# Half of the last group's first layer, and a quarter of group 7's, by seven products of halves

## The chip, the core and the metric

The kernel runs on one core of a Trainium2 chip. Time is device microseconds of one execution; the profile is of one execution, taken by the hardware profiler. PE is TensorE (PEld are its weight loads), DVE is VectorE, ACT is ScalarE, POOL is GpSimd, SP is SyncE, which here issues DMAs.

## What is computed

Attention with a relative bias over 8 batches of 8 heads, 576 positions of 64 elements, and after it a feed-forward layer with a squared ReLU over the 4608 resulting rows of 512 elements:

```python
scores = scale * np.matmul(q, k.transpose(0, 1, 3, 2)) + bias
attn = softmax(scores)
x = np.matmul(attn, v)          # 8 x 8 x 576 x 64, then rows of 512: 4608 x 512
h = np.maximum(x @ w_in, 0.0)   # w_in 512 x 2048
out = h * h @ w_out             # w_out 2048 x 512
```

Inputs and output are float32. On the chip the matmuls take float16 and add up in float32.

## The kernel before

**An order by a planner.** The kernel doesn't emit its instructions as it goes. It first adds operations to a plan (`P.add`), each with an assumed cost per engine, what it depends on, the buffers that it takes from small rings (`Ring`, `Buf`) and a due time. Then the plan is scheduled once as a list, and the instructions are emitted in that order. The assumed costs and due times (`due`) thus decide the order on each engine's queue, but not the time on the chip: there each engine takes its queue from the front and waits on semaphores.

**Attention.** A pair is two heads of one batch (`pair(p)`, 32 of them). Its scores go to the two double banks `st` of PSUM (ring `r_set`, lines 702, 726, 751), ScalarE takes the exponential into one of three `pt` buffers (ring `r_pt`, line 713), VectorE multiplies by the bias' exponentials (line 794), and TensorE multiplies by v into the single bank `pv` (ring `r_pv`, lines 830 and 837). VectorE normalises into `x` (lines 854 and 859), and from batch 2 on SP turns x with a DMA into `xt`, where the 512 elements lie on partitions in four chunks (line 875). Each pair does so in two parts, of three and of two tiles of positions.

**The feed-forward layer.** It works on nine groups of 512 rows (`layers(g)`, g from 0 to 8). Group 7 needs the first part of batch 7's four pairs, group 8 needs all, so both come after the last scores.
- Layer 1 has 16 blocks, one for every 128 hidden columns (`f1`, line 1102): four matmuls, one per chunk of the 512 elements, each with 512 moving columns (the rows of x), into one of three banks `f` (ring `r_g`). ScalarE takes the ReLU of a block into one of four `rt` buffers (line 1123), VectorE squares it into `g` (line 1133), of which there are two, taken in turn by the groups.
- Layer 2 (`second(g)`, line 1017) already computes a product of two matrices split in halves each way by seven products instead of eight (Winograd's form of Strassen's scheme). VectorE makes the sums of g (line 972); a product is 2 x 8 matmuls with 256 moving columns; the results are gathered by VectorE in four float32 buffers `y` (line 1045, or a ScalarE copy, line 1051) and written out by SP (line 1073).
- `layers(g)` puts layer 1 of group g between the products of layer 2 of group g - 1: block i of layer 1 is due at `due + i * 2000`, a step of layer 2 1000 later (and another 7000 later in group 8).

**Buffers with a second use.** `fs`, two float32 buffers, take v in float32 for later batches; `stg`, the staging buffers of q and k, take the loaded pairs. All of that is done when group 7 begins.

Of the kernel before, what the change touches and what calls it, by code (L numbers as in the profile page):

```python
# [11 lines left out]
FP16 = mybir.dt.float16  # L12
EXPF = mybir.ActivationFunctionType.Exp
RELUF = mybir.ActivationFunctionType.Relu
COPYF = mybir.ActivationFunctionType.Copy
MULT = mybir.AluOpType.mult

# [8 lines left out]
GT = 512  # L26
# [13 lines left out]
SIX = 2  # L40
V_EARLY, V_HW = 18900.0, 2
LATE2 = 7000
T_POOL, T_DUE = 0, 0
ORDER = "k0 i0 q1 q0 v i1 o0 k1 i2 o1 o2 i3 o3"
HALF = GT // 2
# [135 lines left out]
def mm(n):  # L181
    return n / 2.4 + 2.5
# [6 lines left out]
def dve(n, rate=1.0, fix=160.0):  # L189
    return fix + n / (0.96 * rate)  # L190
# [3 lines left out]
def kernel(  # L194
# [13 lines left out]
    def io(ins):  # L208
        tc.keep_in_program_order(ins)
        return ins  # L210
# [399 lines left out]

    xt_ready, x_last = {}, {}
    x_bufs = {}

    def copy_to(engs_n, out_f, in_f, deps, bufs, due, fp16=True, dve_only=False):

# [13 lines left out]
    def pair(p):  # L629
# [63 lines left out]
        def run(jts):  # L693
            sets = [Buf(r_set) for _ in jts]

            def score():
                kt, qt = kts[qb.slot], qts[qb.slot]
                for jt, st in zip(jts, sets):
                    for e in range(2):
                        rw = ds(64 * e, 64)  # L700
                        io(
                            nc.tensor.matmul(  # L702
                                sets_ps[st.slot][:, e, :], kt[rw, ts(jt, 128)], qt[rw, 0:512],
                                start=True, stop=True,
                            )
                        )

            o = P.add({"PE": len(jts) * mm(512) + 10}, score, evac, sets + [qb, pb], T, after, "r")
            for jt, st in zip(jts, sets):

                def ex(jt=jt, st=st):
                    io(
                        nc.scalar.activation(  # L713
                            out=p5(pts[pb.slot])[:, jt, :, 0:512], in_=sets_ps[st.slot], func=EXPF, scale=SCALE
                        )
                    )

                exps[jt] = P.add({"ACT": act(1024)}, ex, [o], [st, pb], T)
# [214 lines left out]
    def sums_of_weights():  # L933
# [21 lines left out]
            done.append(o)  # L955
        return done

    def sums_of_activations(g):

        gb = g_bufs[g]  # L960
        sb_ = s_bufs[g] = {i: Buf(r_s[i]) for i in (1, 2, 4)}
        for c0 in (0, 4):
            o = None
            for to, uses in ((1, [1]), (2, [1, 2]), (4, [2, 4]), (3, [])):

                def add(to=to, c0=c0):
                    a11, a12, a21, a22 = (fourth(gb, eo, t, c0, 4) for t in range(2) for eo in range(2))
                    s = {i: ss[i][:, c0 : c0 + 4] for i in (1, 2, 4)}
                    out_, a, b_ = {
                        1: (s[1], a21, a22), 2: (s[2], a11, s[1]), 4: (s[4], a12, s[2]), 3: (a21, a21, a11)  # L970
                    }[to]
                    io(nc.vector.tensor_tensor(out=out_, in0=a, in1=b_, op=mybir.AluOpType.subtract))  # L972

                o = P.add(
                    {"DVE": dve(1024, 2.0)}, add, squares[g][2 * c0 : 2 * c0 + 8] + [o],
                    [gb] + [sb_[i] for i in uses], G0 + GP * g - 5e4,
                )
                s_done.setdefault((g, to), []).append(o)

    def second(g):  # L980
# [25 lines left out]
        for i in (int(x) for x in (P_LAST if g == NG - 1 else P_ORDER).split()):  # L1006
            bk, left, right, ns = prod[i]
            own = bk == "e" and g == NG - 1
            home = pv_ps if own else g_ps
            apart = bk == "d" and g == NG - 1  # L1010
            for s_ in range(2):
                bf = bank[f"d{s_}" if bk == "d" else bk]

                def mul(i=i, s_=s_, bf=bf, left=left, right=right, apart=apart, own=own, home=home):
                    for c in range(8):
                        io(
                            nc.tensor.matmul(  # L1017
                                home[bf.slot][:, ts(s_, HALF)], left(c, s_), right(c),
                                start=(c == 0 and (s_ == 0 or apart) and (own or i not in before)), stop=(c == 7),
                                skip_group_check=True,  # L1020
                            )
                        )

                def atom(d, i=i, s_=s_, bf=bf, ns=ns, mul=mul, own=own):
                    deps = d + [x for n in ns for x in s_done[g, n]] + squares[g]
                    deps += read_of[before[i]] if i in before and not own else []
                    deps += l_wout if i in (1, 2) else t_done
                    return P.add(
                        {"PE": 8 * mm(HALF)}, mul, deps, [bf, gb] + [sb_[n] for n in ns if n != 3], 1e6, 0.0, "f",
                    )  # L1030

                atoms.append(atom)
                if s_ == 0 and not apart:
                    continue

                def fin(o, i=i, bf=bf, s0=s_ if apart else 0, n=1 if apart else 2, own=own, home=home):
                    to, plus, where = reads[i]
                    plus = "u" if own else plus
                    cs = ds(s0 * HALF, n * HALF)

                    def ev():
                        dst, ps = ys[y[to].slot][:, cs], home[bf.slot][:, cs]
                        if plus is not None:
                            io(
                                nc.vector.scalar_tensor_tensor(  # L1045
                                    out=dst, in0=ps, scalar=OSC, in1=ys[y[plus].slot][:, cs], op0=MULT,
                                    op1=mybir.AluOpType.add,
                                )
                            )
                        elif e.eng == "ACT":  # L1050
                            io(nc.scalar.activation(out=dst, in_=ps, func=COPYF, scale=OSC))  # L1051
                        else:
                            io(nc.vector.tensor_scalar_mul(out=dst, in0=ps, scalar1=OSC))

                    deps = [o]
                    if plus == "u":
                        deps += read_of[1 if i in (2, 6) else 6]
                    if i == 6 and g == NG - 1:
                        deps += read_of[2]
                    if plus == "v":  # L1060
                        deps += read_of[5]
                    if i == 4:
                        deps += read_of[3] + read_of[5]
                    bufs = [bf, y[to]] + ([y[plus]] if plus not in (None, to) else [])
                    engs = {"DVE": dve(n * HALF)} if plus is not None else {"DVE": dve(n * HALF), "ACT": act(n * HALF)}
                    e = P.add(engs, ev, deps, bufs, 0.0)
                    read_of.setdefault(i, []).append(e)
                    if where is not None:
                        t, h = where
                        P.add(  # L1070
                            {"SP": 640.0},
                            lambda: io(
                                nc.sync.dma_start(
                                    out=rows_[t][:, s0 : s0 + n, ts(h, HALF)],
                                    in_=ys[y[to].slot][:, cs].rearrange("p (s d) -> p s d", s=n),
                                )
                            ),
                            [e], [y[to]], 0.0,
                        )

                atoms.append(fin)
        return atoms

    def layers(g):

        due = G0 + GP * g
# [2 lines left out]
        if g < NG:  # L1089
            g_bufs[g] = Buf(r_gb)  # L1090
            gb1 = g_bufs[g]
            squares[g] = []
            for nt in range(16):
                bank = Buf(r_g)

                def f1(nt=nt, bank=bank):
# [10 lines left out]
                            )  # L1107

                atoms1.append((nt, f1, bank))
        i2 = 0  # L1110
        last = None
        for i in range(16):
            if i < len(atoms1):
                nt, f1, bank = atoms1[i]
                o = P.add(
                    {"PE": 4 * mm(512)}, f1, xt_ready[g] + [l_win[nt // 4]], [bank, gb1], due + i * 2000, 0.0, "f"
                )
                f1_last[g] = o
                rb = Buf(r_rt)
# [1 line left out]
                def relu(o, bank=bank, rb=rb):  # L1121
# [4 lines left out]

                engs = {"ACT": act(512), "DVE": dve(512)} if g < RELU_DVE else {"ACT": act(512)}
                r = one_of(engs, relu, [o], [bank, rb], 0.0)
                squares[g].append(
                    P.add(  # L1130
                        {"DVE": dve(512, 2.0)},
                        lambda rb=rb, nt=nt, gb1=gb1: io(
# [64 lines left out]
```

## Time and profile before

| | us |
|---|---|
| median of four runs | 373.31 |
| the four runs | 372.51 to 373.9 |
| the profiled execution | 373.9 |
| its span | 372.1 |

The span is what the profiler records between first and last instruction; the rest of an execution's time lies around it. Busy time by stretch, in us:

| stretch | PE | weight loads | VectorE | ScalarE | GpSimd |
|---|---|---|---|---|---|
| 0 to 80 | 67.8 | 42.8 | 63.9 | 66.6 | 57.3 |
| 80 to 160 | 78.6 | 53.2 | 56.6 | 56.7 | 48.7 |
| 160 to 240 | 80.0 | 56.6 | 58.2 | 60.8 | 51.3 |
| 240 to 316 | 76.0 | 54.3 | 54.6 | 52.7 | 26.8 |
| 316 to 372.1 | 53.0 | 35.4 | 31.1 | 20.9 | 0 |

The last row is the part in which only layer 1 of groups 7 and 8 and layer 2 of groups 7 and 8 are left. Its three us without TensorE are the last reads, the last write and the program's end. The granted clock is full but for the last two us, where TensorE has nothing to do.

A row of groups reads: line, engine, operation, output<-input with shapes, count | busy us, mean ns of one | idle time of the engine before it, and what ended most of that. A matmul's mean there is from its start to its modelled end, and they overlap; what one costs in a row of them is the distance of their starts.

### The profile page before, as it was taken

What the parts mean: (1) busy time and instruction counts of PE and PEld (TensorE: products, weight loads), DVE (VectorE), ACT (ScalarE), POOL (GpSimd) and SP (SyncE); (2) the same over time, 40 slices, a digit from 0 to 9 for tenths busy, and PEclk for the clock granted to TensorE, in tenths of its full rate; (3) what the DMA queues carried; (4) which work ended last, traced back from release to release, by engine and by line L of the source; (5) the groups of instructions that cost most, each with busy time, mean ns of one, the idle gap of its engine ahead of it and who ended that gap; (6) DMA issues with size and microseconds to landing.
All of it is one profiled execution on the core that took longest, in us unless ns stands there. A gap on an engine that the chain in (4) does not pass through costs nothing.

```text
span 372.1 us, 9910 instructions
## 1 busy us (share of the span) xinstructions
PE 355.4 (96%) x3930; PEld 242.4 (65%) x3930; DVE 264.3 (71%) x594; ACT 257.6 (69%) x367; POOL 184.0 (49%) x343
## 2 busy tenths in 40 slices
PE   3978999899998999999999999999999999999996
PEld 2656455556686557877785468745876688546785
DVE  3897789867775588658965687669765885483673
ACT  4998989688574887689766887688659870574220
POOL 8898359294655676656846557667623000000000
PEclk9999999999999999999999999999999999999999
DMA  9999999595999999999999899999975112200022
GB/s 171 151 126 161 200 179 94 94 115 100 175 128 124 149 158 114 131 154 163 121 128 155 108 161 122 149 167 138 121 114 130 47 43 50 85 2 28 30 84 86
DMA packets 162292, 44.25 MB, mean 119 GB/s; under 512 B 145734, under 2 KB 162246, under 8 KB 162246
## 3 DMA queue, kind: packets, MB, share of 16 engines
q0 software_dynamic: 74208, 14.53, 51.7%
q1 hardware_dynamic: 87696, 28.80, 40.5%
q8 instruction: 31, 0.51, 0.6%
q10 hardware_dynamic: 342, 0.30, 0.3%
q14 instruction: 15, 0.12, 0.1%
HBM read 36.88 MB, written 9.44 MB: 124 GB/s over the span
## 4 chain that ended last, share of the span: by engine, by line
PE 87%; DVE 7%; DMA 3%; ACT 2%; issue 1%; ACTq 0%; DVEq 0%
PE f L1102 34%; PE f L1017 28%; PE pv L837 9%; PE st L702 8%; PE pv L830 3%; PE st L751 2%; DVE pt L794 2%; DMA xt<-x 2%; PE st L726 1%; DVE x L859 1%; DMA g<-in_q_dram 1%; PE f L657 1%; ACT pm L761 1%; DVE s L972 1%; PE f L359 1%
## 5 line engine op out<-in xcount | busy, mean ns | idle before, releaser
L713 ACT ACTIVATE pt<-st 128x1024 f16<-128x1024 f32 x128 | 127.4, 1023 | 30.8 <-PE st L702 30.7
L1102 PE MATMUL f<-xt,w_in_sb 128*128 128x512 f16 (+4 forms) x704 | 138.7, 341 | 1.4 <-DMA xt<-x 1.2
L1123 ACT ACTIVATE rt<-f 128x512 f16<-128x512 f32 x144 | 85.2, 601 | 50.5 <-PE f L1102 45.4
L1102 PEld LDWEIGHTS <-w_in_sb 128*128 128x128 f16 x704 | 62.6, 98 | 57.3 <-issue 12.7
L1133 DVE TENSOR_TENSOR g<-rt 128x512 f16<-128x512 f16 x144 | 63.5, 446 | 37.7 <-ACT rt L1123 36.9
L794 DVE TENSOR_TENSOR pt<-pt,tb_sb 128x1536 f16<-128x1536 f16 (+2 forms) x96 | 59.7, 631 | 14.9 <-ACT pt L713 14.1
L1017 PEld LDWEIGHTS <-g 128*128 128x128 f16 x576 | 54.5, 98 | 14.5 <-issue 4.7
L276 POOL DMA_DIRECT2D qs<-in_q_dram x79 | 55.4, 715 | 5.0 <-DMA w_out_sb<-in_moe_w_out_dram 2.6
L276 POOL DMA_DIRECT2D ks<-in_k_dram x79 | 55.4, 704 | 1.5 <-issue 1.3
L837 PE MATMUL pv<-va,pt 128*128 128x65 f16 x1280 | 54.7, 193 | 0.0
L837 PEld LDWEIGHTS <-pt 128*128 128x128 f16 x1280 | 50.2, 97 | 3.2 <-issue 1.3
L1017 PEld LDWEIGHTS <-s 128*128 128x128 f16 x432 | 41.2, 98 | 11.1 <-issue 4.0
L1045 DVE SCALAR_TENSOR_TENSOR y<-f,y 128x512 f32<-128x512 f32 (+1 forms) x47 | 31.4, 667 | 23.4 <-PE f L1017 23.0
L702 PE MATMUL st<-qt,kt 64*128 64x512 f16 x256 | 40.7, 389 | 0.9 <-ACT pt L736 0.4
L684 POOL COPY qz<-kt 64x64 f16<-64x64 f16 x58 | 17.2, 297 | 44.6 <-DMA kt<-ks 36.1
L684 POOL COPY qz<-qt 64x64 f16<-64x64 f16 x61 | 19.6, 322 | 37.0 <-DMA qt<-qs 25.9
L830 PE MATMUL pv<-vm,pm 128*128 128x130 f16 x160 | 35.3, 221 | 1.1 <-DVE x L859 1.0
L1017 PE MATMUL f<-wt,g 128*128 128x256 f16 x288 | 36.2, 273 | 0.0
L1017 PE MATMUL f<-w_out_sb,s 128*128 128x256 f16 x288 | 36.1, 273 | 0.0
L1017 PE MATMUL f<-w_out_sb,g 128*128 128x256 f16 x272 | 34.5, 273 | 0.7 <-ACT y L1051 0.7
L859 DVE TENSOR_TENSOR x<-pv,r 128x384 f16<-128x384 f32 x64 | 31.4, 491 | 2.0
L972 DVE TENSOR_TENSOR s<-g,s 128x1024 f16<-128x1024 f16 x36 | 25.6, 712 | 0.4
(66 smaller groups left out, 283.9 us busy)
## 6 DMA issues: line engine op xcount, KB each, us to landing
out_dram<-y SPq DMA_DIRECT2D x34, 256.0 KB, 2.3
f<-in_v_dram SPq DMA_DIRECT2D x24, 256.0 KB, 4.2
qs<-in_q_dram POOLq DMA_DIRECT2D x48, 64.0 KB, 4.3
ks<-in_k_dram POOLq DMA_DIRECT2D x48, 64.0 KB, 3.5
w_in_sb<-in_moe_w_in_dram POOLq DMA_DIRECT2D x4, 512.0 KB, 7.9
w_out_sb<-in_moe_w_out_dram POOLq DMA_DIRECT2D x4, 512.0 KB, 11.6
qs<-in_q_dram POOLq DMA_DIRECT2D x7, 144.0 KB, 4.7
ks<-in_k_dram POOLq DMA_DIRECT2D x7, 144.0 KB, 6.2
```

The source lines that it names most:

```text
L276: lambda: io(eng.dma_start(out=out_(), in_=in_())),
L684: io(eng.tensor_copy(out=dst[qb.slot][rw, rw], in_=src[qb.slot][rw, 512:576]))
L702: nc.tensor.matmul(sets_ps[st.slot][:, e, :], kt[rw, ts(jt, 128)], qt[rw, 0:512], start=True, stop=True,)
L713: nc.scalar.activation(out=p5(pts[pb.slot])[:, jt, :, 0:512], in_=sets_ps[st.slot], func=EXPF, scale=SCALE)
L794: io(nc.vector.tensor_tensor(out=a, in0=a, in1=t, op=MULT))
L830: nc.tensor.matmul(ps[:, i, :, :], pm[:, c : c + 128], vm[:, hp, :, 0:65], start=True, stop=False)
L837: nc.tensor.matmul(ps[:, i, e, :], pt[:, (2 * jt + e) * S + c : (2 * jt + e) * S + c + 128], va[:, jt, 2 * hp + e, 0:65], start=False, sto ...
L859: nc.vector.tensor_tensor(out=xs[xb.slot][:, qt0 : qt0 + nq, :].rearrange("p t (e d) -> p t e d", e=2), in0=ps[:, :, :, 0:64], in1=rs[rb.s ...
L1017: nc.tensor.matmul(home[bf.slot][:, ts(s_, HALF)], left(c, s_), right(c), start=(c == 0 and (s_ == 0 or apart) and (own or i not in before ...
L1102: nc.tensor.matmul(g_ps[bank.slot][:, a:z], w_in_sb[:, kk, ts(nt, 128)], xt_sb[:, kk, c : c + z - a], start=(kk == 0), stop=(kk == 3),)
L1123: io(nc.scalar.activation(out=rts[rb.slot], in_=g_ps[bank.slot], func=RELUF))
L1133: nc.vector.tensor_tensor(out=gs[gb1.slot][:, nt, :], in0=rts[rb.slot], in1=rts[rb.slot], op=MULT)
```

## The change

The 2048 hidden columns are taken as two halves of 1024, and each half as four pieces of 256. A unit u is piece u of both halves, for one group: the four blocks 2u, 2u + 1, 8 + 2u and 9 + 2u. Group 7 computes one unit by seven products, group 8 two; the other blocks (12 and 8) stay as they were.

In a unit the 512 elements are split in halves (k), the 512 rows in halves (j), and the columns by half of the hidden layer (i). VectorE makes four sums of the group's x (`t`, once for a group, into the staging buffers of q and k) and four sums of w_in (`s_`, once for each u, into a `pt` buffer that the plan takes after the last scores). A product is four matmuls with 256 moving columns. The seven go to four banks: 1 and then 2 on top of it into one of the double banks `st`, 6 into an `f` bank, 5 and then 3 on top of it into `pv`, 7 and then 4 into the other `st`. Before a product is added to a bank, the value that the bank holds is read (ScalarE copies 1; VectorE reads 6, 5, 7, 3 and 4 and adds a float32 buffer, an `fs` or a `y`, to each). Four of the reads give quarters of the unit: 2 (read with the ReLU by ScalarE) and 7, 3 and 4 (written by VectorE to `rt`, where ScalarE takes the ReLU in place). The square of a quarter is made by VectorE or ScalarE, as the plan chooses.

`squares[g]` becomes a list for each block, so that the sums for layer 2 wait for their own blocks. Remaining blocks d of a group with units are due at `place(d)`.

```diff
+UNITS = {7: 1, 8: 2}
+AT = (0, 0.5, 2, 2.5, 4, 5.5, 7)
...
+    def made(g, a, z):
+        return [x for nt in range(a, z) for x in squares[g][nt]]
...
-                    {"DVE": dve(1024, 2.0)}, add, squares[g][2 * c0 : 2 * c0 + 8] + [o],
+                    {"DVE": dve(1024, 2.0)}, add, made(g, 2 * c0, 2 * c0 + 8) + [o],
...
+    def sum_of_w(i, u):
+        return pts[late["room"].slot][:, ts(i - 1, 1024)].rearrange("p (k c) -> p k c", k=2)[:, :, ts(u, 256)]
+    def late_sums(n, dst, terms, deps, due, bufs=()):
+        o, made_ = None, []
+        for i, (a, b_, op) in terms:
+            o = P.add(
+                {"DVE": dve(n, 2.0)},
+                lambda i=i, a=a, b_=b_, op=op: io(nc.vector.tensor_tensor(out=dst(i), in0=a(), in1=b_(), op=op)),
+                deps + [o], bufs, due,
+            )
+            made_.append(o)
+        return made_
+    def by_sevens(g, units, due):
...
+        wq = lambda i, k, u: w_in_sb[:, 2 * k : 2 * k + 2, 1024 * i + 256 * u : 1024 * i + 256 * u + 256]
+        xq = lambda k, j: xt_sb[:, 2 * k : 2 * k + 2, c + HALF * j : c + HALF * j + HALF]
+        o_ = 4 * (g - min(UNITS)) - 1
+        t = lambda i: stg[(i + o_) // 2][(i + o_) % 2][:, 0:512].rearrange("p (k c) -> p k c", k=2)
+        t_ops = late_sums(
+            512, t,
+            [
+                (1, (lambda: xq(0, 1), lambda: xq(0, 0), SUB)),
+                (2, (lambda: xq(1, 1), lambda: t(1), SUB)),
+                (4, (lambda: xq(1, 0), lambda: t(2), SUB)),
+                (3, (lambda: xq(1, 1), lambda: xq(0, 1), SUB)),
+            ],
+            xt_ready[g], due - 1e5,
+        )
+        for u in range(units):
+            s_ = lambda i, u=u: sum_of_w(i, u)
+            if ("ops", u) not in late:
+                late["ops", u] = late_sums(
+                    512, s_,
+                    [
+                        (1, (lambda u=u: wq(1, 0, u), lambda u=u: wq(1, 1, u), mybir.AluOpType.add)),
+                        (2, (lambda s_=s_: s_(1), lambda u=u: wq(0, 0, u), SUB)),
+                        (4, (lambda u=u: wq(0, 1, u), lambda s_=s_: s_(2), SUB)),
+                        (3, (lambda u=u: wq(0, 0, u), lambda u=u: wq(1, 0, u), SUB)),
+                    ],
+                    l_win + last_scores, due + 10.0 * u, [late["room"]],
+                )
+            banks = {"a": Buf(r_set), "b": Buf(r_g), "c": Buf(r_pv), "d": Buf(r_set)}
+            y = {"u": Buf(r_f), "v": Buf(r_y)}
+            prod = {
+                1: ("a", lambda u=u: wq(0, 0, u), lambda: xq(0, 0), True),
+                6: ("b", lambda s_=s_: s_(2), lambda: t(2), True),
+                2: ("a", lambda u=u: wq(0, 1, u), lambda: xq(1, 0), False),
+                5: ("c", lambda s_=s_: s_(1), lambda: t(1), True),
+                7: ("d", lambda s_=s_: s_(3), lambda: t(3), True),
+                3: ("c", lambda s_=s_: s_(4), lambda: xq(1, 1), False),
+                4: ("d", lambda u=u: wq(1, 1, u), lambda: t(4), False),
+            }
+            after_read = {2: 1, 3: 5, 4: 7}
+            for n, i in enumerate((1, 6, 2, 5, 7, 3, 4)):
...
+                    for f in range(2):
+                        for kk in range(2):
+                            io(nc.tensor.matmul(ps()[:, ts(f, HALF)], left()[:, kk, ts(f, 128)], right()[:, kk, :], ...))
+                o = f1_last[g] = P.add(
+                    {"PE": 4 * mm(HALF)}, mul,
+                    xt_ready[g] + t_ops + late["ops", u] + (read_of[after_read[i]] if i in after_read else []),
+                    [st, gb1, late["room"]], due + (8 * u + AT[n]) * 2000.0, 0.0, "f",
+                )
...
+                e = one_of({"DVE": dve(512) + 100.0} if plus else {"ACT": act(512) + 100.0}, ev, deps, bufs, 0.0)
...
+                        lambda rb=rb: io(nc.scalar.activation(out=rts[rb.slot], in_=rts[rb.slot], func=RELUF)),
...
+                e = one_of({"DVE": dve(512, 2.0), "ACT": act(512)}, square, [e], [rb, gb1], due - 1e5)
...
-            for nt in range(16):
+            units = UNITS.get(g, 0)
+            for nt in [nt for nt in range(16) if nt % 8 >= 2 * units]:
...
+            def place(d):
+                return 2 * d + 1 if d < 4 * units else 4 * units + d
```

In the order of instructions everything stands as before up to the last attention rows of the last pairs. From there the new order differs on TensorE, VectorE, ScalarE and SP. On TensorE: the two halves of one product of group 6's layer 2, which stood on either side of some attention rows or blocks of group 7, stand together; group 7's first block comes after both halves of product 4; the seven products of a unit stand among the blocks and the layer-2 products. On SP: the DMA that turns the first part of pair 31 stands behind that of the second part of pair 30.

## What is predicted

> **What bounds the kernel now.** I read the page's busy line and slices first, then the chain that ended last, then that chain's pieces in order of time, then the rows of the instructions that the change touches.
>
> ```profile
> PE 355.4 (96%) x3930; PEld 242.4 (65%) x3930; DVE 264.3 (71%) x594; ACT 257.6 (69%) x367; POOL 184.0 (49%) x343
> ...
> PE   3978999899998999999999999999999999999996
> ...
> PEclk9999999999999999999999999999999999999999
> ...
> PE 87%; DVE 7%; DMA 3%; ACT 2%; issue 1%; ACTq 0%; DVEq 0%
> ```
>
> TensorE is busy without a hole from the fourteenth slice to the last but one, at the full granted clock. Being busy isn't yet being at its own limit, so I look at what one matmul costs in the last 60 us, where both changed groups lie (the chain in order of time: start, length, what):
>
> ```profile
> 315.19 0.86 PE f L1102 x4
> ...
> 319.53 14.68 PE f L1102 x68
> ...
> 348.10 1.75 PE f L1017 x16
> ...
> 360.29 8.75 PE f L1017 x80
> ```
>
> A 512-wide matmul of layer 1 takes 14.68/68 = 215.9 ns; a 256-wide one of layer 2 takes 8.75/80 = 109.4 ns. Each piece begins where the one before it ends, so from 313 us to 369.04 us TensorE issues without a wait. What is left after that, the last read, its DMA and the end of the program, isn't touched. In this stretch a change of the time is the change of TensorE's work plus any wait that it gains.
>
> **What is removed.** A unit is 256 columns of each half of the hidden layer for one group: four blocks of L1102, 16 matmuls of 512, 16 x 215.9 = 3.454 us. In its place stand seven products of four 256-wide matmuls: 28 x 109.4 = 3.063 us. One unit saves 0.39 us; one unit in group 7 and two in group 8 save **1.18 us**, all of it on the path.
>
> At this term a rule speaks against the change. A 256-wide matmul has as many weights to load as a 512-wide one, so a unit's loads go from 16 to 28. The trace's row for a load is 98 ns (L1017 and L1102 alike), and layer 2's pieces of eight loads and eight matmuls take 0.87 us: a fresh load every 109 ns is hidden whole. The Trainium skill, "TensorE: Matmul & The Clock Gate", section "Part 3: Packing small matmuls — row/col tiling", says that a weight load overlaps running matmuls only when it goes to another row group. All these take all 128 rows; by that rule a unit would cost 28 x (98 + 109.4) = 5.81 us against 16 x (98 + 215.9) = 5.02 us, a loss of 0.79 us a unit and 2.4 us in all. The L1017 pieces are the same shape as the new products (128 x 128 weights, 256 moving columns), so I take the row: +1.18 us gained. The rule is kept as a rival.
>
> **What is added on VectorE and ScalarE.**
>
> ```profile
> L1123 ACT ACTIVATE rt<-f 128x512 f16<-128x512 f32 x144 | 85.2, 601 | 50.5 <-PE f L1102 45.4
> L1133 DVE TENSOR_TENSOR g<-rt 128x512 f16<-128x512 f16 x144 | 63.5, 446 | 37.7 <-ACT rt L1123 36.9
> ...
> L1045 DVE SCALAR_TENSOR_TENSOR y<-f,y 128x512 f32<-128x512 f32 (+1 forms) x47 | 31.4, 667 | 23.4 <-PE f L1017 23.0
> ```
>
> In the last 54 us each ReLU waits for its matmuls 0.27 us and more: the readers have room. From the timeline I take starts: a matmul group's reader starts 0.20 us after the group's last issue slot (316.09 after 315.89); two ACTIVATEs of 512 in a row start 0.48 us apart (two take 1.09 us together at 14.28), I take 0.50; a VectorE product of 512 halves holds the engine 0.34 us (0.42 long), a 1024 one 0.61 (0.69), and a PSUM read with an added tensor 0.60 (0.69); ScalarE to VectorE takes 0.03.
> - Twelve ReLUs leave ScalarE; three copies, three ReLUs from PSUM, nine ReLUs in place and nine squares come, and two copies of layer 2 go over to VectorE: ten ACTIVATEs more, 10 x 0.5 = 5.0 us.
> - VectorE gets 8 sums of x, 8 of w_in, 15 reads with an added tensor and those two copies, and loses nine squares: 7 x 0.34 + 17 x 0.60 = 12.6 us. It is busy 31.1 of the last 54 us (the windows from 316 us on), so 44 after.
>
> None of it is on TensorE, so its price is only what makes TensorE wait. I followed the new queue orders, engine by engine, with those spacings.
>
> *First unit* (zero at the first block of group 7; TensorE slots: blocks 0.86, products 0.44). Three blocks to 2.59; products 1, 6, 5, 7, 2 to 4.77; two blocks to 6.50; products 3, 4 to 7.37; then blocks end at 8.24, 9.10, 9.96. Product 2 adds to product 1's bank and must wait for the copy of 1: read from 3.29, done 3.89, wanted 4.34: 0.4 us spare. Product 3 waits for VectorE's read of 5 (3.92 + 0.61 + 0.69 = 5.2), wanted 6.50; product 4 for that of 7 (5.8), wanted 6.94. ScalarE then has nine in a row: ReLU of 2 at 4.97, its square at 5.60 (it waits for that ReLU), and seven more at 0.50 each, the last, at 9.10, the ReLU of the block that ended at 8.24. It ends 9.70; the block at 9.96 wants that bank: **0.2 us spare, the tightest wait of all**. Five of the nine read SBUF. In-place ReLU and square aren't in the trace. Near row: the one ACTIVATE from SBUF (L477, 768 elements) took 0.843 us where the PSUM rows' line gives 0.174 + 768/1200 = 0.814, so 0.03 more each, 5 x 0.03 = 0.15: still covered. Far end: if none of the nine overlapped (0.63 apart), 8 x 0.13 - 0.2 = 0.8 us lost. The new program has one table load, as before, so a square adds no switch of tables. Below nothing there is no room, TensorE having no wait to give back. I take 0 for it, by L477.
>
> *Sums of w_in* (eight, 0.34 each, before the last attention rows): they stand between the normalisations of the last pairs. The next pv waits for those, and before it TensorE now runs 16 layer-2 matmuls in one piece (1.75 us) where the chain shows 8 (0.87). The normalisation takes 0.2 + 0.2 + 0.56, with two sums ahead of it 1.64: covered. Without that cover it would cost the two sums' 0.68.
>
> *Transposes of x.* On SP the first part of pair 31 now stands behind the second of pair 30: 1.19 us later, issued at about 312.3 (311.08 before), landed 3.3 us on, at 315.6, and 0.3 more for the sum ahead of it. The first block is itself 1.75 us later (both halves of product 4 stand before it), at 316.9. Covered by 1.0. VectorE's sums of x wait for the same landing, and behind them a read of layer 2 that frees the bank of the third block: product 4 ends at 316.9, read by 317.8, wanted at 318.7. The outputs on SP keep their order at the end.
>
> *The end.* Product 6 of the last group needs the sums of squares. Let E be the end of the last block. TensorE then runs 16 + 16 + 16 matmuls and wants the sums at E + 5.25 (E + 4.37 before, when they were done 1.4 early: 358.93 against 360.29). VectorE: a read of group 7's that ends at E + 2.55 stands in its queue first, then 0.61 (g), 0.67, 0.69: E + 4.5, **0.7 us spare**.
>
> Sum: -1.18 + 0. On the profiled execution, 373.9 us (span 372.1 us and 1.8 around it), that gives 372.7; that execution lay 0.6 above the median of the four runs, 373.31, and the forecast for a median is 373.31 - 1.18 = **372.1 us**.
>
> **Rivals.**
> - *Part of it is given back.* The 0.2 and 0.4 us above are eaten: the far end costs 0.8 in the first unit; units two and three have layer-2 pieces of 0.87 and 1.75 us between their products, so less, say 0.4 together by the same spacing. For it: nine ACTIVATEs in a row where the trace has one each 0.86 us. Against it: L477, and L371's overlap. Time: 372.5 to 373.3, middle 372.9.
> - *VectorE becomes the bound in the last group* (the other side). From the first product of group 8 to E TensorE has 8 blocks, 14 products and 96 matmuls of layer 2, 23.5 us; VectorE has 16 reads of PSUM (9.6), 11 squares (3.7) and 8 large sums (4.9) in it, 18 us, where it had 11.4 of the 22 us from 334 to 356. It is first in, first out, so a read that waits for its product holds everything behind it. Each us by which it is later than 0.7 us at E + 5.25 stops TensorE; at 1.9 us late the whole saving is gone. 3.5 us late: +2.8 - 1.18, so 374.9. For it: chains of reads, each adding to the last. Against it: five us idle in the stretch, and reads that TensorE's order puts 0.4 to 2 us apart.
> - *The weight loads show*, by the rule above: 373.31 + 2.4 = 375.7; decided where a matmul of the products takes over 3.454/28 = 123 ns. L1017's 109.4 speaks against it.
> - That the change doesn't do what it says is out: 36 more matmuls stand in the new order, 84 of 256 columns for 48 of 512.
>
> **Chances.** Forecast 0.70, part given back 0.12, VectorE 0.14, loads 0.04. About 0.3% (1.12 us) can be told from no change, so the bound lies at 372.19, right at the forecast. The runs lie -0.8 to +0.6 around their median: I give 0.43 of the forecast's 0.70 to faster and 0.27 to no change; part given back adds 0.12 there; the other two are slower. Range 371.5 (the forecast less most of that scatter) to 373.8 (all given back, with scatter); most of the 0.18 lies above it.
>
> **What would show it.** Right: products at 109 ns a matmul, no wait of TensorE on ScalarE or VectorE after 313 us, and the last matmul 1.2 us earlier. Wrong: TensorE waiting at the ninth block or at product 2 on ScalarE (first rival); before product 6 of the last group on VectorE's sums (second); product matmuls over 123 ns (third). A saving above 1.3 us would mean that waits which I don't see in this trace went.

## The result and the profile after

The changed kernel takes 372.21 us (median of 43 runs, 370.94 to 374.89), the kernel before 373.04 on the same chips (64 runs, 371.71 to 374.66). The ratio is 0.9972 with a 95% interval of 0.9963 to 0.9981: 1.04 us less, between 0.7 and 1.4; the two medians lie 0.83 apart, which is inside it. In some executions the mean granted clock is 0.995 instead of 1.00 and the time about 1.1 us longer (15 of the changed kernel's 44, median 372.83 us against 371.71), so a ratio moves with their share on either side, while the stretch that the change touches ran at 1.00 in every trace. The profiled span went from 372.1 to 370.6 us.

The page of the changed kernel, its busy line, TensorE's slices, the shares of the chain that ended last, and the rows that answer to L1123, L1133 and L1045 of before:

```profile
PE 354.2 (96%) x3966; PEld 245.9 (66%) x3966; DVE 277.4 (75%) x618; ACT 262.7 (71%) x377; POOL 185.9 (50%) x343
...
PE   3988999899999999999999999999999999999996
...
PE 86%; DVE 7%; DMA 3%; ACT 2%; issue 1%; POOL 0%; SPq 0%; ACTq 0%; DVEq 0%
...
L1286 ACT ACTIVATE rt<-f 128x512 f16<-128x512 f32 x132 | 77.7, 601 | 38.4 <-PE f L1257 34.4
...
L1296 DVE TENSOR_TENSOR g<-rt 128x512 f16<-128x512 f16 x132 | 58.7, 449 | 21.1 <-ACT rt L1286 20.0
...
L1056 DVE SCALAR_TENSOR_TENSOR y<-f,y 128x512 f32<-128x512 f32 (+1 forms) x47 | 31.4, 668 | 24.2 <-PE f L1028 24.0
```

TensorE has 36 matmuls more and is busy 1.2 us less. VectorE is busy 13 us more and ScalarE 5 us more, and still TensorE's slices stay at 9 from the ninth to the last but one. Twelve blocks less go through the ReLU and the square of the blocks (144 to 132). The chain in order of time (start, length, what) tells whether TensorE waits:

```profile
302.32 0.54 PE st L707 x4
...
316.65 2.59 PE f L1257 x12
319.24 0.44 PE st L1182 x4
319.68 0.44 PE f L1182 x4
320.11 0.44 PE pv L1182 x4
320.55 0.87 PE st L1182 x8
321.42 1.73 PE f L1257 x8
...
353.57 3.49 PE f L1028 x32
357.06 1.75 PE pv L1028 x16
358.81 8.75 PE f L1028 x80
```

Each piece begins where the one before it ends, the products (L1182) too: four matmuls take 0.44 us, eight 0.87, which is 109 ns each. After 303 us TensorE waits for no other engine, as before.

The chain sets the start of a piece at the modelled end of the matmul before it. That end lies behind the start of the next matmul, as the timeline of TensorE's own instructions shows:

```profile
316.49 2.75 PE L1257 MATMUL f<-xt,w_in_sb 128*128 128x512 f16 x12
...
323.86 6.21 PE L1257 MATMUL f<-xt,w_in_sb 128*128 128x512 f16 x28
```

The chain has these two at 316.65 and 324.02, 0.16 later. Between two places of the chain this drops out. Where a start of TensorE is set against the end of another engine's instruction, the timeline's start counts.

One measure is used from here on, the **tail**: from the start of the last four matmuls of the scores (302.32 here, 302.60 before) to the end of the last matmul (358.81 + 8.75 = 367.56; before 360.29 + 8.75 = 369.04), both by the chain. The start in the chain of before:

```profile
302.60 0.54 PE st L702 x4
```

Profiled executions also differ by some tenths of a us in what lies ahead of it, where these edits change nothing. The tail was 66.44 us and is 65.24: 1.20 us less. The other 0.3 us between the two spans lies ahead of it.

### The profile page after: what moved, and what is told of

Its sections match the earlier page's. It is cut to its first block, busy times and chain, and to the rows that moved or that the text cites. A ratio compares the mean times of both kernels' runs of the same rounds, so it can differ in the third digit from the quotient of the medians.

```text
span 370.6 us, 10030 instructions
## 1 busy us (share of the span) xinstructions
PE 354.2 (96%) x3966; PEld 245.9 (66%) x3966; DVE 277.4 (75%) x618; ACT 262.7 (71%) x377; POOL 185.9 (50%) x343
## 4 chain that ended last, share of the span: by engine, by line
PE 86%; DVE 7%; DMA 3%; ACT 2%; issue 1%; POOL 0%; SPq 0%; ACTq 0%; DVEq 0%
PE f L1257 32%; PE f L1028 28%; PE pv L844 8%; PE st L707 8%; PE pv L837 2%; PE st L758 2%; DMA kt<-ks 2%; DVE pt L801 2%; PE st L733 2%; PE st L1182 1%; DVE x L866 1%; DMA g<-in_q_dram 1%; PE f L662 1%; ACT pm L768 1%; PE pv L1182 1%
## 5 line engine op out<-in xcount | busy, mean ns | idle before, releaser
L1257 PE MATMUL f<-xt,w_in_sb 128*128 128x512 f16 (+4 forms) x656 | 127.8, 338 | 0.2 <-ACT xt L624 0.2
L1286 ACT ACTIVATE rt<-f 128x512 f16<-128x512 f32 x132 | 77.7, 601 | 38.4 <-PE f L1257 34.4
L1257 PEld LDWEIGHTS <-w_in_sb 128*128 128x128 f16 x656 | 57.9, 98 | 52.1 <-issue 12.2
L1296 DVE TENSOR_TENSOR g<-rt 128x512 f16<-128x512 f16 x132 | 58.7, 449 | 21.1 <-ACT rt L1286 20.0
L689 POOL COPY qz<-kt 64x64 f16<-64x64 f16 x58 | 18.2, 314 | 38.1 <-DMA kt<-ks 29.5
L983 DVE TENSOR_TENSOR s<-g,s 128x1024 f16<-128x1024 f16 x36 | 25.9, 720 | 0.4
```

Of the source, the lines that this page charges most:

```text
L689: io(eng.tensor_copy(out=dst[qb.slot][rw, rw], in_=src[qb.slot][rw, 512:576]))
L1257: nc.tensor.matmul(g_ps[bank.slot][:, a:z], w_in_sb[:, kk, ts(nt, 128)], xt_sb[:, kk, c : c + z - a], start=(kk == 0), stop=(kk == 3),)
L1286: io(nc.scalar.activation(out=rts[rb.slot], in_=g_ps[bank.slot], func=RELUF))
L1296: nc.vector.tensor_tensor(out=gs[gb1.slot][:, nt, :], in0=rts[rb.slot], in1=rts[rb.slot], op=MULT)
```

## The experiments

The ratio is to the kernel before, with its 95% interval; the tail is of one profiled execution, beside the 66.44 us of before (e8's chain doesn't pass the last scores; there the tail starts at 301.74, where the matmul ahead of them ends).

| run | what | median us | ratio | tail us |
|---|---|---|---|---|
| after | the change | 372.21 | 0.9972 (0.9963 to 0.9981) | 65.24 |
| e1_wide256 | before, blocks of groups 7 and 8 in 256 columns | 373.8 | 1.002 (1.0007 to 1.0033) | 66.75 |
| e2_wide128 | the same in 128 columns | 373.86 | 1.0029 (1.0012 to 1.0046) | 67.39 |
| e3_relu_twice | after, in-place ReLUs twice | 374.18 | 1.0014 (0.9995 to 1.0034) | 67.20 |
| e4_sums_twice | after, two of the last sums twice | 372.62 | 0.9989 (0.9976 to 1.0002) | 65.90 |
| e5_only8 | two units in group 8, none in 7 | 372.8 | 0.999 (0.997 to 1.0009) | 65.63 |
| e6_two_two | two units in each | 374.31 | 1.0032 (1.0017 to 1.0048) | 66.99 |
| e7_one_three | one in 7, three in 8 | 375.37 | 1.0061 (1.0047 to 1.0074) | 68.07 |
| e8_two_four | two in 7, four in 8 | 378.64 | 1.0154 (1.0136 to 1.0172) | 72.19 |
| e9_spread_one_three | as e7, other due times | 371.02 | 0.9937 (0.9917 to 0.9957) | 63.72 |
| e10_spread_one_two | as after, due times of e9 | 371.37 | 0.9941 (0.9924 to 0.9959) | 64.12 |
| e11_change_again | the change, beside e9 and e10 | 371.81 | 0.9949 (0.993 to 0.9968) | 65.25 |

My theory was the prediction's: TensorE's own work sets this stretch, a matmul costs its moving columns, and VectorE and ScalarE are covered. The rivals were that fresh weights cost time, and that the readers of PSUM stop TensorE.

### Fresh weights alone: e1 and e2

In the kernel before, the blocks of groups 7 and 8 are cut into matmuls of 256 or 128 columns. The weights are loaded two or four times as often; the results are the same.

```diff
-                    for a, z, c in ((0, n, c), (n, GT, 0)):
+                    cut = [(0, n, c), (n, GT, 0)]
+                    if g >= 7:
+                        cut = [(a, a + 256, c + a) for a in range(0, GT, 256)]
+                    for a, z, c in cut:
```

> The kernel before, with the 32 blocks of layer 1 of groups 7 and 8 computed in two runs of four matmuls of 256 columns instead of one run of four of 512: 256 weight loads there instead of 128, the same columns, and no other change. Theory (a fresh load every 109 ns is hidden): a block takes 8 x 109.4 = 0.875 us instead of 0.864, +0.4 us in all, ratio about 1.001. Rival (loads don't overlap running matmuls when they take the same rows): 128 more loads of 98 ns show, +12.5 us, ratio 1.034.

> As the run with 256 columns, with four runs of 128 columns to a block: 512 weight loads instead of 128. If a load's 98 ns in the profile is time that the next load must wait, a matmul takes 98 ns: 512 x 98 = 50.2 us for 27.6, +22.5 us, ratio 1.06. If loads follow each other faster than they last, as four scores' matmuls of 128 columns take 0.22 us in the chain: 512 x 55 ns = 28.2 us, +0.6 us, ratio 1.0015. The theory behind the prediction needs neither; it holds if the 256 run is right. I expect the second.

The tail grew by 0.31 us with 256 columns and by 0.95 with 128. The rows by form of e1 between 319 and 334 us, matmuls and loads:

```profile
L1105 PE MATMUL f<-xt,w_in_sb 128*128 128x256 f16 x135 | 14.9, 273 | 0.0
L1105 PEld LDWEIGHTS <-w_in_sb 128*128 128x128 f16 x132 | 12.9, 98 | 1.5
```

and of e2 in the same window:

```profile
L1105 PE MATMUL f<-xt,w_in_sb 128*128 128x128 f16 x265 | 15.0, 219 | 0.0
L1105 PEld LDWEIGHTS <-w_in_sb 128*128 128x128 f16 x262 | 14.7, 98 | 0.0
```

A load is 98 ns in both. In e1, 135 matmuls fit in 15 us, and 265 in e2, about 56 ns each, less than one load's row: loads run beside matmuls and beside one another. By the prediction's distances, 128 fresh loads more should cost the difference between 2 x 109.4 and 215.9 ns, 0.37 us in all, and e1 shows no more than that. The rival of the weight loads falls.

### ScalarE's cover: e3

Every in-place ReLU of the products is done twice; a ReLU of a ReLU is the same value.

```diff
-  lambda rb=rb: io(nc.scalar.activation(out=rts[rb.slot], in_=rts[rb.slot], func=RELUF)),
+  lambda rb=rb: [
+      io(nc.scalar.activation(out=rts[rb.slot], in_=rts[rb.slot], func=RELUF)) for _ in range(2)
+  ],
```

> The changed kernel with each of the nine in-place ReLUs made twice (the second changes nothing), the orders otherwise the same. Theory (the readers are hidden with little to spare in group 7's unit): three more ACTIVATEs, 1.5 us, stand before the ReLU that the ninth block waits for, which had 0.3 us to spare in the changed kernel's trace: TensorE waits 1.1 us there, +0 to 0.5 in the other two units; +1.1 to 1.6 us against the changed kernel, that is 0 to +0.5 us against the kernel before, ratio 1.000 to 1.0015. Rival (ScalarE has room to take this up, its queue empties before any bank is wanted): the saving stays, ratio 0.997.

The tail is 1.96 us longer than that of the change, more than expected. First ScalarE's timeline in the changed kernel (start, length, line, what):

```profile
322.63 0.58 ACT L1286 ACTIVATE rt<-f 128x512 f16<-128x512 f32 x1
323.11 0.62 ACT L1221 ACTIVATE rt<-rt 128x512 f16<-128x512 f16 x1
323.63 0.59 ACT L1286 ACTIVATE rt<-f 128x512 f16<-128x512 f32 x1
324.10 0.63 ACT L1230 ACTIVATE g<-rt 128x512 f16<-128x512 f16 x1
324.62 1.14 ACT L1221 ACTIVATE rt<-rt 128x512 f16<-128x512 f16 x2
325.66 1.59 ACT L1286 ACTIVATE rt<-f 128x512 f16<-128x512 f32 x3
```

Then the same stretch of e3, and TensorE's waits of e3 after 300 us (line, for whom: us in total, times, longest):

```profile
322.53 1.28 ACT L1222 ACTIVATE rt<-rt 128x512 f16<-128x512 f16 x2
...
324.72 2.46 ACT L1222 ACTIVATE rt<-rt 128x512 f16<-128x512 f16 x4
327.09 2.29 ACT L1288 ACTIVATE rt<-f 128x512 f16<-128x512 f32 x4
```
```profile
PE f L1259 <- ACT rt L1288: 1.7, 1, 1.7
```

The ninth block waits for the first ReLU of that last line, where the prediction put the tightest wait. Three in-place ReLUs stand ahead of it. In the changed kernel they take 0.52 (323.11 to 323.63) and 1.04 us (324.62 to 325.66), in e3 1.19 (322.53 to the next start at 323.72) and 2.37 (324.72 to 327.09): 2.0 us more, 0.67 each instead of the 0.5 I had used. A second ReLU, which reads what the first wrote, doesn't overlap it (the two take 1.28 us), while independent ACTIVATEs start 0.47 to 0.54 apart. TensorE around this wait in e3:

```profile
327.72 3.61 PE L1259 MATMUL f<-xt,w_in_sb 128*128 128x512 f16 x16 [1.67 <-ACT rt L1288]
331.17 0.60 PE L1182 MATMUL st<-xt,w_in_sb 128*128 128x256 f16 x4
```

The sixteen matmuls are listed with 3.61 us, but the next starts 3.45 us after them: the modelled end is 0.16 late. The listed wait, 1.67, counts from such an end, so from start to start TensorE loses 1.83 us of the 2.0: the cover was 0.2 us. With 0.13 more in the last piece of layer 2 (8.88 us by the chain for 8.75), whose cause stays open, that is the tail's 1.96.

### VectorE's cover at the end: e4

Two of the last group's sums of squares, ahead of product 6, are made twice, with the same results.

```diff
-  io(nc.vector.tensor_tensor(out=out_, in0=a, in1=b_, op=mybir.AluOpType.subtract))
+  for _ in range(2 if g == NG - 1 and c0 == 4 and to in (1, 2) else 1):
+      io(nc.vector.tensor_tensor(out=out_, in0=a, in1=b_, op=mybir.AluOpType.subtract))
```

> The changed kernel with the first two sums of squares of the last group's second half made twice by VectorE (the second changes nothing), the orders otherwise the same. Theory: product 6 of the last group needs them; in the changed kernel's trace the second is done at 358.21 and the first weight load of the product starts at 358.54, so 0.33 us to spare. 0.61 + 0.67 = 1.28 us more makes TensorE wait 0.8 to 0.95 us: ratio to the kernel before 0.9995. Rival (the end isn't set by these sums, there is more cover than the trace shows): no loss, ratio 0.997.

TensorE's weight loads around product 6 in e4, and its one wait after 300 us:

```profile
355.93 2.83 PEld L1029 LDWEIGHTS <-g 128*128 128x128 f16 x26
358.77 0.42 PEld L1029 LDWEIGHTS <-s 128*128 128x128 f16 x4
359.96 2.95 PEld L1029 LDWEIGHTS <-s 128*128 128x128 f16 x28 [0.77 <-DVE s L984]
```
```profile
PE f L1029 <- DVE s L984: 0.5, 1, 0.5
```

and the loads in the changed kernel:

```profile
358.54 3.48 PEld L1028 LDWEIGHTS <-s 128*128 128x128 f16 x32
```

The tail grew by 0.66, less than expected. The expectation had counted to the first load of product 6. That was the wrong place: four loads read the sums of the other half of the columns (`c0` 0), and only the fifth waits, as the break after "x4" shows. The sums of the changed kernel:

```profile
357.53 1.42 DVE L983 TENSOR_TENSOR s<-g,s 128x1024 f16<-128x1024 f16 x2
```

The needed sum is the first of these two, done at 358.21, and the fifth load comes four matmuls after 358.54, at 358.98: 0.77 us of cover. The needed sum's end moves from 0.33 us ahead of the first load to 1.14 after it (359.91 against 358.77; its second copy starts at 359.21 in e4's chain and takes 0.70), 1.47 later, and 0.77 of that shows at the load: 0.70 of cover by this count. What TensorE's matmuls lose, the tail's 0.66, is the listed 0.5 and again the 0.16 of the modelled end.

### How many units: e5 to e8

`UNITS` alone says how many units a group has; for three or four, the sums of w_in take a second `pt` buffer.

```diff
-UNITS = {7: 1, 8: 2}
+UNITS = {8: 2}          # e5
+UNITS = {7: 2, 8: 2}    # e6
+UNITS = {7: 1, 8: 3}    # e7
+UNITS = {7: 2, 8: 4}    # e8
```

> The change in group 8 alone, two units. Theory (each unit saves 0.39 us of TensorE's work and every read is hidden): -0.78 us, ratio 0.9979. In the trace no wait of TensorE after 313 us. Rival (the saving of the change came mostly from the new places of layer-2 products, not from the products of halves): the ratio doesn't follow the number of units.

> Two units in group 7 and two in group 8. Theory: four units, 4 x 0.392 = 1.57 us of work saved; in group 7, where no layer-2 product stands between, two units need 2 x 7 ACTIVATEs and 8 ReLUs, 11 us of ScalarE in 13 us of TensorE, so the waits at banks grow: 0 to 0.8 us lost. Ratio 0.9958 to 0.998. Rival (readers bound): slower than the changed kernel, ratio over 0.9975.

> One unit in group 7 and three in group 8. Theory: four units, -1.57 us, ratio 0.9958, if VectorE keeps up: from the first product of group 8 on it gets five more reads (3.0 us) and four sums of w_in earlier, in a stretch in which it had five us idle, so I expect 0 to 0.6 us lost before product 6 of the last group: 0.996 to 0.9975. Rival (VectorE becomes the bound): its lateness shows as a wait of TensorE before product 6, over 1 us, ratio over 0.9985.

> Two units in group 7 and all four in group 8. TensorE's work falls by 6 x 0.392 = 2.35 us, ratio 0.9937 if all is hidden. VectorE in group 8: 20 reads (12 us), 8 large sums (4.9), layer-2 reads (4.2) and what squares it takes, some 24 us in 24 us of TensorE's work, so it should be the bound: I expect 1.5 to 4 us of waits before the last group's sums, ratio 0.998 to 1.004.

| | units | TensorE's work by the prediction's 0.39 | tail against before | difference |
|---|---|---|---|---|
| e5 | 2 | -0.78 | -0.81 | 0 |
| after | 3 | -1.18 | -1.20 | 0 |
| e6 | 4 | -1.57 | +0.55 | 2.1 |
| e7 | 4 | -1.57 | +1.63 | 3.2 |
| e8 | 6 | -2.35 | +5.75 | 8.1 |

Two and three units gain what their matmuls save. From four on, with this order, the readers stop TensorE, by far more than I had expected for each of the three. TensorE's waits after 300 us in e6:

```profile
PE f L1257 <- ACT rt L1286: 1.2, 1, 1.2
PE f L1028 <- DVE s L983: 0.6, 1, 0.6
```

in e7:

```profile
PE f L1028 <- ACT g L1230: 1.8, 1, 1.8
PE pv L1182 <- DVE y L1207: 0.3, 1, 0.3
```

and the first of e8's:

```profile
PE f L1028 <- ACT g L1230: 1.7, 1, 1.7
PE pv L1182 <- DVE y L1207: 1.5, 3, 0.8
PE f L1028 <- DVE s L983: 0.9, 1, 0.9
```

They are the two places with least to spare, used up (ScalarE at a block of layer 1, VectorE's sums at the end), and from e7 on a new one: layer 2 waits for the square of a product's quarter. The listed waits come to 1.8 us in e6 (two), 2.5 in e7 (four, the other two of 0.2) and 6.1 in e8 (nine). With the 0.16 that each costs beyond what is listed, as in e3 and e4, that is 2.1 of e6's 2.1 us, 3.1 of e7's 3.2 and 7.5 of e8's 8.1; the last 0.6 of e8 isn't attributed.

### Too much work for the readers, or its place: e9 to e11

In e7's order ten products of the second and third unit stand in a row between 339.6 and 344.5 us, then 32 matmuls of layer 2, then four products, and then layer 2 wants the squares that come from those. Two theories fit e7: VectorE and ScalarE have too much to do, or the same work comes in a heap. e9 has e7's units with other due times: the units of a group are due 4 steps apart instead of 8, so that they overlap and group 8's last product is due at step 15 instead of 23, and block d is due at 1.3 d (group 8's four at 0 to 3.9 instead of 1 to 7). Products, blocks and layer 2's pieces thus come between one another.

```diff
-UNITS = {7: 1, 8: 2}
+UNITS = {7: 1, 8: 3}
...
-    [st, gb1, late["room"]], due + (8 * u + AT[n]) * 2000.0, 0.0, "f",
+    [st, gb1, late["room", u // 2]], due + (0 + 4 * u + AT[n]) * 2000.0, 0.0, "f",
...
-                return 2 * d + 1 if d < 4 * units else 4 * units + d
+                return 1.3 * d
```

> One unit in group 7 and three in group 8, as in the run that lost 2 to 3 us, but with other due times: the units of a group due 4 steps apart instead of 8, and the remaining blocks at 1.3 times their number. In the new order the products of group 8's third unit stand singly between pieces of 8 layer-2 matmuls, where eight products stood in a row. If VectorE's and ScalarE's total work is what bounded that run, this one loses the same, ratio over 1.004. If it was the products in a row (each read by one engine while TensorE is through with the next in 0.44 us), the waits go, and the fourth unit's 0.39 us is gained: -1.57 us from the last scores to the last matmul, ratio 0.9958, at most 0.5 us of waits left. I expect the second, at 0.996 to 0.9975.

> The changed kernel's units, one and two, with the due times of the run with three: what the other order alone does. TensorE had no wait in the changed kernel, so it can't gain: -1.18 us against the kernel before, ratio 0.9968, the same as the changed kernel within 0.1 us from the last scores to the last matmul; if the changed kernel's order hid a loss, up to 0.3 us better.

> The changed kernel once more, on the same chip as the two runs with other due times, so that the three stand side by side: ratio 0.9968 to 0.9975, -1.2 us from the last scores to the last matmul.

The end of the products in e9, in its chain in order of time:

```profile
346.09 0.87 PE f L1028 x8
346.96 0.44 PE st L1182 x4
347.40 1.75 PE f L1028 x16
349.14 0.44 PE pv L1182 x4
349.58 0.87 PE f L1028 x8
350.45 0.44 PE st L1182 x4
350.89 4.37 PE f L1028 x40
```

Single products stand between pieces of layer 2, and each piece begins where the one before it ends. The windows from 345.00 to 365.90 us give busy time and count of TensorE, its loads, VectorE, ScalarE and GpSimd, then the clock; e9:

```profile
345.00:365.90 20.90, 20.74 (x190) 18.34 (x188) 15.33 (x26) 6.69 (x11) 0.00 (x0) 1.00 0.20 68
```

and e7:

```profile
345.00:365.90 20.90, 18.58 (x168) 16.11 (x166) 15.88 (x27) 5.59 (x11) 0.00 (x0) 1.00 0.16 52
```

VectorE and ScalarE do about the same in both, VectorE far from full; TensorE is idle for 2.3 us of it in e7, and 0.2 in e9, after its last matmul at 365.75. e9 has no wait of TensorE after 300 us. One more thing differs: the plan gave six squares of quarters to ScalarE in e9 that VectorE makes in e7 (14 and 2 against 8 and 8). e7's own queues show that work hadn't piled up where its longest wait begins:

```profile
348.49 0.69 DVE L1207 SCALAR_TENSOR_TENSOR y<-pv,f 128x512 f32<-128x512 f32 x1 [0.22 <-PE pv L1182]
350.01 0.63 ACT L1221 ACTIVATE rt<-rt 128x512 f16<-128x512 f16 x1 [2.94 <-DVE rt L1207]
```

VectorE stood idle for the product, and ScalarE, which makes the square that TensorE then waits for, had stood idle for 2.94 us. So for that wait, 1.8 us, it is the place of the work: the product comes too shortly before layer 2 wants its square. How much of e7's shorter waits the six squares would have removed isn't separated. e9's tail is 2.72 us below before, e10's 2.32, but in both orders three attention rows and four matmuls of the scores, 1.11 us together, have moved ahead of the tail's start. Without that it is -1.61 for four units (-1.57 by the sum) and -1.21 for three (-1.18).

e9, e10 and the change ran side by side on one chip. At a clock of 1.00 the medians there are 373.05 us for the kernel before (6 of its 11 executions), 371.02 for e9 and 371.37 for e10 (6 of 6 each) and 371.69 for the change (5 of 6): e9 is 2.0 us below the kernel before, where its ratio would make it 2.4. e9 has the lowest median of all, but its times and those of the change overlap, so that it beats the change rests on the tails (0.4 us of work), not on the times.

## Why the prediction was right

The forecast, 372.1, was -1.18 on the median of before, then 373.31; the measured difference is -1.04 (0.7 to 1.4) on a median of 373.04. The mechanism shows in the trace, where the tail is 1.20 shorter.

- **The saving of a unit, 0.39 us.** Tails with two, three and four units without waits are shorter by 0.81, 1.20 and 1.61: 0.40 each.
- **The weight loads.** The products take 109 ns a matmul, as L1017's row said. The rule of the Trainium skill, "TensorE: Matmul & The Clock Gate", section "Part 3: Packing small matmuls — row/col tiling", that a load overlaps only from another row group, would have made e1 some 12 us longer; it grew by 0.3. For weights of 128 x 128 after each other the measurement decides, against it. The same section also says that a load into a background weight buffer is pulled ahead of running matmuls; the runs agree with that sentence.
- **The readers' added work.** From 316 us to the end VectorE is busy 40.8 us and ScalarE 25.9, 9.7 and 5.0 more than before. Predicted were 12.6 (9.9 without the sums of w_in, 2.7, which stand ahead of that window) and 5.0.

```profile
316.00:370.60 54.60, 51.54 (x394) 38.30 (x392) 40.78 (x77) 25.92 (x45) 0.00 (x0) 1.00 0.15 50
```

- **Operations that the trace of before didn't show.** The in-place ReLU takes 627 ns and the square on ScalarE 630, against 595 for the ReLU from PSUM in the same window: the 0.03 more that L477 gave. The far end, no overlap between them, was wrong: starts in the timeline lie 0.47 to 0.54 apart.
- **The tightest wait.** The ninth block's ReLU was to start at 9.10, end at 9.70 and free the bank for a block at 9.96: 0.2 us to spare. Counted from the first block's own start, 316.49, it started at 9.17 (325.66) and ended at 9.76; the block came at 9.96 (326.45: the start at 323.86 and twelve matmuls). That leaves 0.2, and e3 finds 0.2.
- **Product 2.** The copy of product 1 ended at 320.36, product 2 came at 320.82: 0.46 to spare, predicted 0.4.
- **The landing of x.** The first block stands at 316.65 in the chain (predicted 316.9), its own start is 316.49, and VectorE's first sum of x started at 315.55, so x had landed by then: at least 0.9 us of cover, predicted 1.0. No pv matmul waits either, so the sums of w_in are covered as well.
- **The end.** The size of this cover came out partly by luck. The sums were to be ready at E + 4.5, wanted at E + 5.25. E is 353.40 by the matmuls' own starts; the sums were ready at E + 4.81, 0.3 later than predicted, and product 6 began at E + 5.24 (358.64): 0.4 us to spare and not 0.7. Part of such a miss is visible in the prediction itself: its "1.4 early" sets 358.93, an end on VectorE, against 360.29, a start by the chain (360.12 by the timeline). Making up for it, only the fifth load reads these sums, which the prediction left out; by that load and by e4 the cover is 0.7 to 0.8.
- **The rival on the slower side**, VectorE as the bound in the last group, is real but begins one unit further on: e6 has the forecast wait on VectorE's sums, 0.6 us. That a VectorE instruction holds what stands behind it shows in e3: a sum of x, whose inputs were ready at 322.42, starts at 326.38, behind a square for which VectorE stood idle for 1.27 us until 326.03. But the rival's mechanism was only half right. e8 is stopped with VectorE busy for 21.3 of the 26 us from 340 to 366, and e7 and e9 show how much depends on how the products lie.

What failed are expectations of experiments. For e6, e7 and e8 I scaled the readers' work with the units and took the order's spacing as given; at most 0.8, 0.6 and 4 us of waits were expected, and 2.1, 3.2 and 8.1 came. For e3 I used the spacing of independent ACTIVATEs for dependent ones, and for e4 the first load of a product instead of the first that needs the sum.

Not settled: what makes up the last 0.6 us of e8's loss, how much of e7's shorter waits is the share of work between VectorE and ScalarE, and whether e9's extra unit shows in the time, not only in the trace.

## What to carry to other kernels

Price a scheme with fewer multiplications by the measured distance of matmuls of exactly its shape, then follow every engine's queue through it and write down the spare time at each wait: here 0.2 and 0.7 us of cover decided how many units could be added. Take both ends of such a time from the engines' own instructions: a start taken from the chain was 0.16 us late here. When the cover runs out, look at how the new work lies in the queue before giving up on it: products in a heap cost 3.2 us; as many, spread between layer 2's pieces and with six squares moved to ScalarE, cost nothing.

## What the runs showed of the hardware

Loads of 128 x 128 weights, 98 ns each in their rows, follow one another every 56 ns or so when the matmuls have 128 moving columns (e2). The rows of loads can thus be busy 98% of a window, 14.7 of 15 us, with TensorE still at the pace of its columns: 55.8 ns for 128, 109.4 for 256 and 215.9 for 512. The busy share of weight loads is no bound here.
